# Sums of pooled keys and values move from GpSimd to TensorE, with another order of loads and steps, at the beginning of a fused attention and two-MoE kernel

## The chip, the core and the metric

The kernel runs on one core of one Trainium2 chip. The core has TensorE (PE: matmuls and the transposes made with an identity matrix), VectorE (DVE), ScalarE (ACT), GpSimd (POOL) and SyncE (SP), which here only issues DMAs in the order of its queue. The metric is the time of one execution in microseconds (us); lower is better.

## The reference, cut to what matters

```python
# q, k, v: 8 batches x 8 heads x 576 x 64, float32
k_p = k.reshape(B, H, 72, 8, D).mean(axis=3)      # keys and values averaged over 8 rows
v_p = v.reshape(B, H, 72, 8, D).mean(axis=3)
scores = (1 / sqrt(D)) * q @ k_p^T                # 576 x 72 for each head
attn = exp(scores - max) / (sum + 1e-9)
x = (attn @ v_p), heads side by side              # 4608 x 512
h = x @ w_in                                      # d_ff 2048, weights float64
x = (h * cos(h)) @ w_out
out = (silu(x @ w_gate) * (x @ w_val)) @ w_out2   # d_ff 1536
```

## The kernel before, in words

The kernel is one long instruction stream for each engine. Attention of batch 0 stands at the beginning; the first MoE runs over nine blocks of 512 tokens, and the attention of batches 1 to 7 is woven into its slots; the second MoE follows. A slot is one piece of 128 columns of the first MoE's d_ff: TensorE makes `h` (`pe_h`, L479 to L481), ScalarE and VectorE make h·cos(h) from it (`turns` and `cosine`; the last step is VectorE's `w`, L516), and TensorE adds it, two slots later, to `acc` (`pe_y`, L542 in block 0). Slot 0 of block 0 is called h_0 and w_0, and so on.

The weights come as float64 and are made into float32 on the chip. A unit (512 columns of 128 rows of `w_in`, or 128 rows of `w_out`) is loaded into `st_i` or `st_o` (L410) and goes through five VectorE steps: `cv_exp` (L417), `cv_sign` (L428), `cv_high` (L434), `cv_low` (L439) and `cv_mul` (L445); a unit of `w_in` has a sixth, the low part of `wa` (L959). (0,0) to (0,3) are the four units that h_0 to h_3 need, (1,0) to (1,3) those of h_4 to h_7, and so on. `fill(n)` puts n such steps into the stream; while block 0 runs, the converted units are consumed soon after they are made.

Attention of batch 0 goes over five tiles of up to 128 queries: `qT` (transposed queries, L241), scores `s` (TensorE, L253), their maximum `mx` (L257), `Exp` on ScalarE, `pm` (the normalized weights, L289 to L302), `pt` and `px` (their transposes on TensorE, L310, L314) with what VectorE makes of them, `ptl` (L312) and `ptx` (L316), and `av` (L330), whose result fills the `ring` that h_0 reads. `do_av` for group 0 (tiles 0 and 1) and group 1 (tiles 2 and 3) stand ahead of h_0.

The averages of 8 rows are sums of halves (`pool_sum`, L186 and L188: 8 rows to 4, to 2, to 1). Keys of batch 0 (`kst`) are summed on VectorE; values of batch 0 (`vst`, one tile of 128 x 5 x 512), keys and values of batch 1 (tiles `k_0`..`k_3`, `v_0`..`v_4`) and keys and values of all later batches (`kraw`, `vraw`, two buffers) on GpSimd. Sums give `kp` and `vp`; `prep_k` transposes `kp` into `kT`, `prep_v` splits `vp`.

The order of all this is written out by hand: a string `program` of steps for what is ahead of h_0 (s0 is `do_s` of tile 0, x0 its normalization, p0 `do_pt`, a0 `do_av` of group 0, m1 one GpSimd sum of batch 1, f4 four conversion steps, i1 and o1 a load of a unit, k and v `prep_k(1)` and `prep_v(0)`, X the split of the ring), and tables of slots after it.

Of the kernel before, what the change touches and what calls it, by code (L numbers as in the profile page):

```python
# [25 lines left out]
def fused_kernel(  # L26
# [216 lines left out]
    def do_s(b, t, e=None):  # L243
        n = TILES[t][1]
        qT = qTs.pop((b, t))
        if e is None:
            e = p1a.tile([P, H, SP], F32, name=f"e_{b}_{t}", tag="e")
        es[b, t] = e
        for hf in range(2):
            ps = psum.tile([P, 4, SP], F32, name=f"s_{b}_{t}_{hf}", tag="att", bufs=2)  # L250
            for j in range(2):
                p = 2 * hf + j
                nc.tensor.matmul(  # L253
                    ps[:n, 2 * j : 2 * j + 2].rearrange("p a b -> p (a b)"), qT[:, p], kT[:, p], start=True, stop=True
                )
# [755 lines left out]

    raw = iter(range(H + NP + 1))

    def more(m):
        for _ in range(m):
            i = next(raw, None)
            if i is not None:
                do_raw(1, i)
# [200 lines left out]
```

## Time and profile before

| what | us |
|---|---|
| median of 3 runs (1805.85 to 1807.25) | 1806.39 |
| the profiled execution | 1807.21 |
| its span, from the first to the last instruction | 1805.5 |
| TensorE busy in the span | 1721.2 (95%) |
| VectorE busy | 1284.0 (71%) |
| ScalarE busy | 1072.8 (59%) |
| GpSimd busy | 211.0 (12%) |

The profiled execution took 1.7 us more than its span, and 0.8 us more than the median. Busy shares are means over a kernel whose stretches differ: the first slices of the profile have TensorE busy at two to five tenths and VectorE at six to nine; from the fourth slice on TensorE stands at nine tenths or more. In the rows below, a name in square brackets behind an arrow is what ended the idle time before the instruction.

### The profile page before, as it was taken

How to read it: one execution, taken by the hardware profiler on the slowest of the kernel's cores; microseconds unless marked ns; L12 is line 12 of the kernel's file. 1: busy time of each engine (PE TensorE's matmuls, PEld its weight loads, DVE VectorE, ACT ScalarE, POOL GpSimd, SP SyncE). 2: the span in 40 equal slices, each digit the busy share in tenths (PEclk: the TensorE clock that was granted, in tenths of full speed). 3: DMA queues.
4: the chain of work that ended last, by engine and by line, in shares of the span. 5: the costliest groups of instructions: out<-in, count | busy, mean ns of one | idle time of the engine just before them, and what ended most of it. 6: DMA issues, size and time to landing. Idle time of an engine off the chain costs nothing.

```text
span 1805.5 us, 23613 instructions
## 1 busy us (share of the span) xinstructions
PE 1721.2 (95%) x8084; PEld 1443.0 (80%) x8084; DVE 1284.0 (71%) x2196; ACT 1072.8 (59%) x1947; POOL 211.0 (12%) x293
## 2 busy tenths in 40 slices
PE   2589999999999999999999999999999999999998
PEld 2455777788878888878878787888888888999998
DVE  6989988877777777787876586863584368358446
ACT  3567787777877777778676564533443344344333
POOL 4371423304104013000000000000000000000000
PEclk9699999999999999999999999999999999999999
DMA  9833356445656454574785488576667557777773
GB/s 188 182 104 92 102 180 196 147 137 180 169 178 224 135 192 138 165 230 150 235 272 178 153 322 288 192 249 228 197 199 268 189 196 219 293 261 248 293 251 93
DMA packets 248160, 357.04 MB, mean 198 GB/s; under 512 B 149608, under 2 KB 155752, under 8 KB 248040
## 3 DMA queue, kind: packets, MB, share of 16 engines
q1 hardware_dynamic: 224540, 351.99, 61.1%
q10 hardware_dynamic: 23500, 3.54, 1.4%
q8 instruction: 65, 1.06, 0.2%
q14 instruction: 55, 0.45, 0.1%
HBM read 285.74 MB, written 69.73 MB: 197 GB/s over the span
## 4 chain that ended last, share of the span: by engine, by line
PE 66%; DVE 18%; DMA 7%; ACT 6%; issue 2%; SPq 1%; POOL 0%; ACTq 0%; DVEq 0%; POOLq 0%
PE X L734 14%; PE oX L864 8%; PE Y L734 7%; PE acc L550 4%; PE acc L551 4%; PE oY L864 4%; PE acc L549 4%; PE h L479 4%; PE h L481 4%; PE h L480 4%; PE Z L734 3%; PE oZ L864 2%; DVE w L516 2%; DVE w L491 2%; PE av L330 1%
## 5 line engine op out<-in xcount | busy, mean ns | idle before, releaser
L479 PE MATMUL h<-xhl,wa 128*128 128x512 f32 x576 | 230.8, 401 | 5.6 <-ACT hs L488 5.6
L734 PE MATMUL X<-t_P,wc 128*128 128x512 f32 (+1 forms) x1080 | 233.5, 368 | 2.6 <-ACT u L783 2.5
L480 PE MATMUL h<-xhl,wa 128*128 128x512 f32 x576 | 226.6, 393 | 0.0
L481 PE MATMUL h<-xhl,wa 128*128 128x512 f32 x576 | 225.3, 391 | 0.0
L734 PEld LDWEIGHTS X<-t_P,wc 128*128 128x128 f32 x1080 | 196.3, 188 | 30.2 <-ACT u L783 5.2
L550 PE MATMUL acc<-gl,wo_ring 128*128 128x512 f32 x448 | 175.8, 392 | 2.3 <-DVE gl L530 2.3
L549 PE MATMUL acc<-gh,wo_ring 128*128 128x512 f32 x448 | 174.7, 400 | 1.0 <-ACT gh L527 0.9
L551 PE MATMUL acc<-gh,wo_ring 128*128 128x512 f32 x448 | 174.9, 390 | 0.0
L516 DVE SCALAR_TENSOR_TENSOR w<-w,hs 128x512 f32<-128x512 f32 x144 | 103.2, 716 | 45.7 <-ACT w L513 44.4
L479 PEld LDWEIGHTS h<-xhl,wa 128*128 128x128 f32 x576 | 108.7, 189 | 29.6 <-ACT hs L488 6.5
L512 ACT ACTIVATE w<-w 128x512 f32<-128x512 f32 x144 | 91.0, 632 | 67.3 <-DVE w L491 66.1
L488 ACT ACTIVATE hs<-h 128x512 f32<-128x512 f32 x144 | 85.7, 595 | 73.8 <-DVE w L516 49.9
L480 PEld LDWEIGHTS h<-xhl,wa 128*128 128x128 f32 x576 | 108.6, 189 | 23.8 <-issue 1.9
L481 PEld LDWEIGHTS h<-xhl,wa 128*128 128x128 f32 x576 | 108.6, 188 | 23.4 <-issue 0.7
L530 DVE TENSOR_TENSOR gl<-w,gh 128x512 fp32r<-128x512 f32 x133 | 96.5, 725 | 38.6 <-ACT gh L527 36.9
L786 DVE TENSOR_TENSOR p<-p,X 128x512 f32<-128x512 f32 (+1 forms) x60 | 37.8, 632 | 116.6 <-PE X L734 109.2
L491 DVE SCALAR_TENSOR_TENSOR w<-w,hs 128x512 f32<-128x512 f32 x144 | 106.3, 738 | 15.9 <-ACT w L490 15.7
L126 ACT CAST xhl<-pst 128x1024 fp32r<-128x1024 f32 (+1 forms) x70 | 67.7, 968 | 71.3 <-PE oX L864 26.1
L490 ACT ACTIVATE w<-hs,few 128x512 f32<-128x512 f32 x144 | 104.6, 726 | 6.2 <-DMA w_dram<-ce_w 4.8
L186 POOL TENSOR_TENSOR kraw<-kraw 72x256 f32<-72x256 f32 x96 | 85.4, 890 | 168.6 <-DMA kraw<-in_k_dram 164.8
L527 ACT CAST gh<-w 128x512 fp32r<-128x512 f32 x133 | 81.7, 615 | 35.6 <-DVE w L516 31.9
L864 PE MATMUL oX<-xhl,wc 128*128 128x512 f32 (+1 forms) x480 | 102.8, 368 | 0.0
(194 smaller groups left out, 3664.6 us busy)
## 6 DMA issues: line engine op xcount, KB each, us to landing
wc<-wc_dram SPq DMA_DIRECT2D x273, 512.0 KB
wo_ring<-wo_dram SPq DMA_DIRECT2D x112, 512.0 KB
wc_dram<-wc SPq DMA_DIRECT2D x42, 512.0 KB
wc_dram<-ow SPq DMA_DIRECT2D x42, 256.0 KB
y_dram<-yo SPq DMA_DIRECT2D x18, 512.0 KB
w_dram<-ce_w SPq DMA_DIRECT2D x36, 256.0 KB
st_i<-in_moe_w_in_dram SPq DMA_DIRECT2D x32, 256.0 KB
st_o<-in_moe_w_out_dram SPq DMA_DIRECT2D x16, 512.0 KB
```

Source lines behind the costliest of these rows:

```text
L479: nc.tensor.matmul(ps, whi, xhl[:, 0, c], start=c == 0, stop=False)
L480: nc.tensor.matmul(ps, whi, xhl[:, 1, c], start=False, stop=False)
L481: nc.tensor.matmul(ps, wlo, xhl[:, 0, c], start=False, stop=c == KC - 1)
L490: nc.scalar.activation(w, h, AF.Identity, bias=magic)
L491: nc.vector.scalar_tensor_tensor(out=w, in0=w, scalar=MAGIC, in1=h, op0=ALU.subtract, op1=ALU.subtract)
L516: nc.vector.scalar_tensor_tensor(out=w, in0=w, scalar=1.0, in1=h, op0=ALU.subtract, op1=ALU.mult, reverse0=True)
L530: nc.vector.tensor_sub(b, w, a)
L549: nc.tensor.matmul(acc[n][i], a[:, cols], xh, start=f == 0, stop=False)
L550: nc.tensor.matmul(acc[n][i], a[:, cols], xl, start=False, stop=False)
L551: nc.tensor.matmul(acc[n][i], b[:, cols], xh, start=False, stop=f == NF1 - 1)
L734: nc.tensor.matmul(ps[:, :hb], w, t[:, x, c, :hb], start=first and c == 0 and n == 0, stop=c == 1 and n == 2, skip_group_check=not first,)
L864: nc.tensor.matmul(banks[key][m][:, :hb], u, x[:, b, i, :hb], start=first_ and j == i == k == 0, stop=j == NJ - 1 and i == 1 and k == 2, s ...
```

## The change

- Values of batch 0 and keys and values of batch 1 are summed by TensorE: matmuls with the identity matrix, which add the eight pieces of 64 columns up in PSUM; ScalarE copies the sums out. In the program these are the steps V0, K and V; V0 stands between the scores of tile 0 and of tile 1, K and V between `av` of group 1 and the scores of tile 4. GpSimd's sums begin with batch 2 (`PEB = 2`).
- The keys get the factor −EXP_SCALE when `prep_k` copies them out of PSUM. So `mx` is a minimum instead of a maximum, the step that multiplied `mx` by −EXP_SCALE on VectorE is gone, and `Exp` has the scale −1.
- The loads have another order (unit (0,1) ahead of the queries, (0,2) ahead of the values of batch 0, (1,0) ahead of the keys of batch 1), and so has the program: conversions of (0,0) and (0,1) stand ahead of the first scores (`fill(6)`, `fill(14)`), conversions go on between the steps with other counts.

```diff
+    PEB = 2
     def load_kv1():
-            for r in range(2):
-                kvraw[1, "k", 2 * p + r] = t[:SP, r]
+            kraw.setdefault(1, []).append(t[:SP])
...
-        nc.scalar.copy(kT[0:64, :, 0:SP], ps[0:64])
-        nc.scalar.copy(kT[64:128, :, SP:], ps[64:128])
+        nc.scalar.mul(kT[0:64, :, 0:SP], ps[0:64], -EXP_SCALE)
+        nc.scalar.mul(kT[64:128, :, SP:], ps[64:128], -EXP_SCALE)
+
+    def sum_k1():
+        new_kp(1)
+        ps = psum.tile([SP, NP, 2, D], F32, name="kps_1s", tag="att", bufs=2)
+        for p, raw in enumerate(kraw[1]):
+            for l in range(POOL):
+                nc.tensor.matmul(
+                    ps[:, p].rearrange("s r d -> s (r d)"), ident[:SP, :SP], raw[:, :, l * D : (l + 1) * D],
+                    start=l == 0, stop=l == POOL - 1,
+                )
+        nc.scalar.copy(kps[1], ps)
+
+    def sum_v(b):
+        new_vp(b)
+        ps = psum.tile([P, NP + 1, D], F32, name=f"vps_{b}", tag="att", bufs=2)
+        for i, raw in vraw[b]:
+            m = raw.shape[1]
+            for l in range(POOL):
+                nc.tensor.matmul(
+                    ps[:, i : i + m].rearrange("p h d -> p (h d)"), ident, raw[:, :, l * D : (l + 1) * D],
+                    start=l == 0, stop=l == POOL - 1,
+                )
+        nc.scalar.copy(vps[b], ps)
...
-            nc.vector.reduce_max(mx[:n, :, 0], ps[:n], axis=AX.X)
+            nc.vector.tensor_reduce(out=mx[:n, :, 0], in_=ps[:n], op=ALU.min, axis=AX.X)
-                nc.vector.tensor_scalar_mul(mx[:n], mx[:n], -EXP_SCALE)
-                        e[:n, h], ps[:n, i], AF.Exp, bias=mx[:n, i], scale=EXP_SCALE, accum_out=sm[:n, h]
+                        e[:n, h], ps[:n, i], AF.Exp, bias=mx[:n, i], scale=-1.0, accum_out=sm[:n, h]
...
-    raws = [(b, kind, i) for b in range(1, B) for kind, m in (("k", H), ("v", NP + 1)) for i in range(m)]
+    raws = [(b, kind, i) for b in range(PEB, B) for kind, m in (("k", H), ("v", NP + 1)) for i in range(m)]
...
+    load_i(1)
     load_q(0)
     load_i(1)
...
+    fill(6)
     new_kp(0)
-    new_vp(0)
-    fill(1)
...
-    pool_sum(nc.gpsimd, vps[0], vst[:, : NP + 1])
+    fill(14)
...
-        "s0 s1 f4 m4 f5 s2 m4 x0 p0 m1 x1 f3 i1 p1 v s3 a0 m1 i1 m2 f12 o7 i2 x2 p2 m1 f5 x3 f4 s4 "
-        "f4 p3 a1 o3 i3 q F3 i1 k o4 X i4 x4 w f4 "
+        "s0 V0 s1 f4 i1 s2 x0 p0 x1 f3 p1 v s3 a0 f6 x2 p2 f3 x3 "
+        "f2 p3 a1 K V1 w i1 F3 X o2 s4 q i2 f8 x4 k b i4 f4 "
```

In the rows of the engines' order below, line numbers are those of each version (L280 of the changed kernel is L253 of before, L234 and L221 are the new sums).

TensorE at the first scores; `s_t_h` is the scores of tile t, half h, `vps` the sum of values of batch 0. Before:

```order
L209 MATMUL kps_159<-ident,kp_148 128x72 x4
L253 MATMUL s_0_0_172<-kT,qT_0_169 128x144 x2
L253 MATMUL s_0_1_183<-kT,qT_0_169 128x144 x2
L253 MATMUL s_1_0_195<-kT,qT_1_193 128x144 x2
L253 MATMUL s_1_1_206<-kT,qT_1_193 128x144 x2
```

Now:

```order
L211 MATMUL kps_170<-ident,kp_163 128x72 x4
L280 MATMUL s_0_0_204<-kT,qT_0_201 128x144 x2
L280 MATMUL s_0_1_214<-kT,qT_0_201 128x144 x2
L234 MATMUL vps_226<-vst,ident 128x320 x8
L280 MATMUL s_1_0_236<-kT,qT_1_223 128x144 x2
L280 MATMUL s_1_1_246<-kT,qT_1_223 128x144 x2
```

Eight matmuls of 320 columns, which need the values of batch 0, have come to stand ahead of the scores of tile 1.

TensorE between the last `av` of group 1 and the first matmuls of h_0. Before:

```order
L330 MATMUL av_1_3_542<-ptx,vl_97 128x256
L209 MATMUL kps_572<-ident,kp_226 128x72 x4
L479 MATMUL h_0_620<-xhl,wa_0_242 128x512
L480 MATMUL h_0_620<-xhl,wa_0_242 128x512
L481 MATMUL h_0_620<-xhl,wa_0_242 128x512
```

Now:

```order
L356 MATMUL av_1_3_462<-ptx,vl_97 128x256
L221 MATMUL kps_1s<-k_0_134,ident 72x128 x8
L221 MATMUL kps_1s<-k_1_136,ident 72x128 x8
L221 MATMUL kps_1s<-k_2_138,ident 72x128 x8
L221 MATMUL kps_1s<-k_3_140,ident 72x128 x8
L234 MATMUL vps_505<-v_0_142,ident 128x128 x8
L234 MATMUL vps_505<-v_2_145,ident 128x128 x8
L234 MATMUL vps_505<-v_4_148,ident 128x64 x8
L280 MATMUL s_4_0_549<-kT,qT_4_357 64x144 x2
L505 MATMUL h_0_627<-xhl,wa_0_179 128x512
L280 MATMUL s_4_1_559<-kT,qT_4_357 64x144 x2
```

All sums of batch 1 (56 matmuls) and the scores of tile 4 have come to stand ahead of h_0 or in its first matmuls; the transposes of the keys of batch 1 went behind its start.

SyncE's queue around the loads of `vraw` of batch 2 and `st_o_5` (the sixth unit of `w_out`). Before:

```order
L160 DMA kraw_7_1222<-in_k_dram 72x512
L163 DMA vraw_0_1280<-in_v_dram 64x512
L410 DMA st_o_4_427<-in_moe_w_out_dram 128x512
L163 DMA vraw_0_1280<-in_v_dram 64x512
L163 DMA vraw_1_1348<-in_v_dram 64x512 x2
L163 DMA vraw_2_1401<-in_v_dram 64x512 x2
L163 DMA vraw_3_1462<-in_v_dram 64x512 x2
L410 DMA st_o_5_429<-in_moe_w_out_dram 128x512
```

Now:

```order
L163 DMA kraw_7_1220<-in_k_dram 72x512
L436 DMA st_o_4_837<-in_moe_w_out_dram 128x512
L166 DMA vraw_0_1280<-in_v_dram 64x512 x2
L166 DMA vraw_1_1350<-in_v_dram 64x512 x2
L166 DMA vraw_2_1407<-in_v_dram 64x512
L436 DMA st_o_5_911<-in_moe_w_out_dram 128x512
L166 DMA vraw_2_1407<-in_v_dram 64x512
L166 DMA vraw_3_1470<-in_v_dram 64x512 x2
```

`st_o_5` now stands behind the first half of `vraw_2`, where it stood behind all of `vraw_3`; the two buffers of `vraw` make the load of `vraw_2` wait for GpSimd's sum of `vraw_0`, that of `vraw_3` for `vraw_1`.

## Rows read from the trace of the kernel before

**Rows 1.** Busy time of each engine by stretch; clock, DMA share, GB/s last.
```profile
core 0: us, PE busy (x) PEld busy (x) DVE busy (x) ACT busy (x) POOL busy (x), PEclk, DMA share, GB/s
28.00:62.00 34.00, 14.12 (x51) 10.96 (x51) 33.23 (x55) 14.34 (x58) 30.20 (x42) 0.94 0.90 176
62.00:82.00 20.00, 9.12 (x38) 7.65 (x39) 18.68 (x42) 10.69 (x35) 1.50 (x2) 0.50 1.03 222
...
140.00:215.00 75.00, 72.14 (x294) 48.50 (x293) 71.73 (x144) 62.26 (x149) 15.39 (x15) 1.00 0.35 96
215.00:1806.00 1591.00, 1572.37 (x7511) 1340.57 (x7509) 1095.33 (x1836) 936.75 (x1586) 125.10 (x181) 1.00 0.63 206
```

**Rows 2.** VectorE's groups by shape, 28 to 62 us: busy us, mean ns.
```profile
L439 DVE SCALAR_TENSOR_TENSOR st_i<-st_i 128x512 f32<-128x512 uint32 x3 | 6.0, 1997 | 0.0
...
L302 DVE COPY pm<-pm 128x64 f32<-128x64 f32 x1 | 2.1, 2060 | 0.0
```

**Rows 3.** The same view, 62 to 94 us.
```profile
L439 DVE SCALAR_TENSOR_TENSOR st_i<-st_i 128x512 f32<-128x512 uint32 x5 | 3.4, 682 | 0.0
...
L302 DVE COPY pm<-pm 64x64 f32<-64x64 f32 x1 | 0.2, 179 | 0.0
```

**Rows 4.** Timeline of GpSimd: start us, us, instructions.
```profile
28.80 4.49 POOL L186 TENSOR_TENSOR vst<-vst 128x1280 f32<-128x1280 f32 x2 [24.32 <-DMA vst<-in_v_dram]
...
117.14 9.56 POOL L186 TENSOR_TENSOR vraw<-vraw 128x256 f32<-128x256 f32 x2 [2.83 <-DMA vraw<-in_v_dram]
```

**Rows 5.** Timeline of VectorE.
```profile
16.77 0.68 DVE L428 SCALAR_TENSOR_TENSOR ce_i<-st_i,ce_i 128x512 uint32<-128x512 uint32 x1
...
78.06 0.68 DVE L439 SCALAR_TENSOR_TENSOR st_i<-st_i 128x512 f32<-128x512 uint32 x1
78.66 0.41 DVE L417 TENSOR_SCALAR wo<-st_o 128x512 uint32<-128x512 uint32 x1
79.00 0.68 DVE L445 SCALAR_TENSOR_TENSOR ce_i<-st_i,ce_i 128x512 f32<-128x512 f32 x1
...
92.70 0.69 DVE L516 SCALAR_TENSOR_TENSOR w<-w,hs 128x512 f32<-128x512 f32 x1
...
106.73 0.94 DVE L516 SCALAR_TENSOR_TENSOR w<-w,hs 128x512 f32<-128x512 f32 x1
...
134.15 0.43 DVE L417 TENSOR_SCALAR wo<-st_o 128x512 uint32<-128x512 uint32 x1 [5.19 <-DMA st_o<-in_moe_w_out_dram]
```

**Rows 6.** Timeline of TensorE.
```profile
76.31 0.58 PE L330 MATMUL av<-pth,vmh 128*128 128x256 f32 x1 [2.23 <-DVE ptl L312]
...
80.32 0.63 PE L330 MATMUL av<-ptx,vl 128*128 128x256 f32 x2
...
81.74 0.77 PE L479 MATMUL h<-xhl,wa 128*128 128x512 f32 x1
...
96.26 3.60 PE L542 MATMUL acc<-w,wo 128*128 128x512 f32 x8
...
107.73 6.19 PE L542 MATMUL acc<-w,wo 128*128 128x512 f32 x8 [4.14 <-DVE w L516]
...
136.52 0.79 PE L479 MATMUL h<-xhl,wa 128*128 128x512 f32 x1 [5.19 <-ACT hs L488]
```

**Rows 7.** Busy time and clock in three stretches that begin with a burst.
```profile
76.30:85.50 9.20, 8.85 (x32) 7.45 (x33) 8.29 (x18) 6.99 (x15) 0.32 (x1) 0.50 0.82 167
...
107.70:112.80 5.10, 5.07 (x6) 2.19 (x7) 5.10 (x7) 2.58 (x4) 4.86 (x6) 0.50 0.16 40
...
136.50:140.10 3.60, 3.25 (x4) 1.46 (x5) 3.57 (x7) 1.98 (x3) 2.89 (x4) 0.50 0.03 11
```

**Rows 8.** What SyncE's queue waited for, 0 to 200 us: total, times, longest.
```profile
SPq L410 <- DMA qi<-in_q_dram: 22.9, 2, 14.7
```

**Rows 9.** Timeline of SyncE's queue.
```profile
113.35 17.08 SPq L163 DMA_DIRECT2D vraw<-in_v_dram  x7
```

More of the change, by code (lines that the diff above doesn't have):

```diff
@@ L149, in fused_kernel @@
     kvraw = {}
+    kraw = {}
+    vraw = {}
     pairs = "(r p) (s l) d -> r s p (l d)"
@@ L179, in load_kv1 @@
                     nc.sync.dma_start(rows[:, 0], vleft[1])
-            for i in range(j, min(j + 2, NP + 1)):
-                kvraw[1, "v", i] = t[:, i - j]
+            vraw.setdefault(1, []).append((j, t[:, : min(2, NP + 1 - j)]))
     def pool_sum(eng, dst, raw):
@@ L205, in prep_k @@
     def prep_k(b):
+        ps = psum.tile([P, NP, SP], F32, name=f"kps_{b}", tag="att", bufs=2)
         kp = kps.pop(b)
-        ps = psum.tile([P, NP, SP], F32, name=f"kps_{b}", tag="att", bufs=2)
         for p in range(NP):
             nc.tensor.transpose(ps[:, p], kp[:, p].rearrange("s r d -> s (r d)"), ident[:SP, :SP])
-        nc.scalar.copy(kT[0:64, :, 0:SP], ps[0:64])
-        nc.scalar.copy(kT[64:128, :, SP:], ps[64:128])
+        nc.scalar.mul(kT[0:64, :, 0:SP], ps[0:64], -EXP_SCALE)
[21 more added lines that the diff above has]
+        nc.scalar.copy(vps[b], ps)
     def prep_v(b):
@@ L273, in do_exp @@
         e = es[b, t][: TILES[t][1]]
-        nc.scalar.activation(e, e, AF.Exp, scale=EXP_SCALE)
+        nc.scalar.activation(e, e, AF.Exp, scale=-1.0)
     def do_norm(b, t, pm=None):
@@ L337, in do_av @@
             done += m
-    raws = [(b, kind, i) for b in range(1, B) for kind, m in (("k", H), ("v", NP + 1)) for i in range(m)]
+    raws = [(b, kind, i) for b in range(PEB, B) for kind, m in (("k", H), ("v", NP + 1)) for i in range(m)]
     def do_raw(b, i):
-        at = (b - 1) * (H + NP + 1) + i
-        if at + 1 < len(raws) and raws[at + 1][0] > 1:
+        at = (b - PEB) * (H + NP + 1) + i
+        if at + 1 < len(raws):
             load_kv(*raws[at + 1])
@@ L979, in fused_kernel @@
     kst4 = kst[:SP].rearrange("s (p r) x -> s r p x", r=2)
+    vraw[0] = [(0, vst[:, : NP + 1])]
     load_i(1)
@@ L1010, in x_ @@
         do_norm(0, t, spare[t][:, NE:] if t % 4 else None)
[L1012 to L1018, printed above, removed]
     program = (
-        "s0 s1 f4 m4 f5 s2 m4 x0 p0 m1 x1 f3 i1 p1 v s3 a0 m1 i1 m2 f12 o7 i2 x2 p2 m1 f5 x3 f4 s4 "
-        "f4 p3 a1 o3 i3 q F3 i1 k o4 X i4 x4 w f4 "
+        "s0 V0 s1 f4 i1 s2 x0 p0 x1 f3 p1 v s3 a0 f6 x2 p2 f3 x3 "
+        "f2 p3 a1 K V1 w i1 F3 X o2 s4 q i2 f8 x4 k b i4 f4 "
     )
@@ L1030, in fused_kernel @@
         "v": lambda: prep_v(0),
-        "m": more,
+        "V": sum_v,
+        "K": sum_k1,
         "f": fill,
@@ L1037, in fused_kernel @@
         "k": lambda: prep_k(1),
+        "b": lambda: load_kv(*raws[0]),
         "w": lambda: wo_raw.extend(
```

## The prediction

> **What bounds the kernel now.** I read first the busy time by stretch [rows 1]. Beyond 215 us TensorE is busy for 1572.4 of 1591 us: an edit at the beginning changes nothing there, except by when that stretch starts. From 140 to 215 us TensorE still has 72.1 of 75. Ahead of it the picture turns: between 28 and 62 us VectorE is busy for 33.2 of 34 us and TensorE for 14.1; between 62 and 82 us VectorE for 18.7 of 20. So up to h_0, which starts at 81.74 us [rows 6], the time is VectorE's, and behind h_0 it is TensorE's with two holes in which it waits for VectorE: 4.14 us ahead of 107.73 for w_1, and 5.19 us ahead of 136.52 [rows 6].
>
> The groups by shape say why VectorE is full. A `cv_low` takes 1997 ns on the mean between 28 and 62 us and 682 ns after it; the copy of 64 columns in `pm` 2060 ns and 179 ns [rows 2, 3]. GpSimd is busy for 30.2 of the 34 us in the first stretch and for 1.5 of 20 in the next, where the DMA share is the higher one, 1.03 against 0.90 [rows 1]. So it is GpSimd's sums, not DMAs, that slow VectorE. Over all 55 instructions the excess over quiet steps comes to some 13 us (an estimate: of the two groups shown, 3.9 and 1.9).
>
> The Trainium skill states this as a rule (SBUF — State Buffer, section "SBUF: two separate sides"): VectorE and GpSimd share one port pair, the pair is locked for a whole instruction, and the loser blocks until it is over. Here the trace agrees: the 2060 ns copy lies under a GpSimd operation of 128x1280, two of which took 4.49 us [rows 4]. By the rule the sums of batch 2, which stay on GpSimd, will still slow VectorE in block 0; the sum below leaves that in by rows anyway.
>
> **The change, step by step, up to av of group 1.** I lay VectorE's new order out at quiet prices: a large step (L439 and its like) 0.60 us from start to start, a small one (L417) 0.34 [rows 5].
>
> - Keys of batch 0 are still summed first; today the next step starts at 16.77 [rows 5]. Then 8 large and 3 small conversion steps (5.8) lead to 22.6, the transposed queries to 23.2, and about 2.2 go by until the first scores and their minima are there. Of the 20 instructions that can run ahead of the scores of tile 1, 8.4 us in all, the last ends at 33.8.
> - These scores now stand behind V0. It needs the values of batch 0, which land at 28.80 [rows 4], and one more 512 KB unit is now loaded ahead of them: 2.6 us at some 200 GB/s (between the 176 and 222 of [rows 1]). So V0 starts at 31.4.
> - Price of V0: 8 x 320 = 2560 columns in float32. `acc` in block 0 is float32 too: four matmuls of 512 columns, each shown as two records, take 3.60 us [rows 6], so 1.76 ns a column at the full clock of 2.4 GHz; at the granted 0.50 that is 3.5. The clock is 0.50 from the start of a burst for 9.2, 5.1 and 3.6 us [rows 7]. If it rises 3.6 us after V0 begins, V0 takes 6.3; if not within it, 9.0. I take 7.5 (rise after the mean, 6 us): V0 ends at 38.9, the first half of the scores 1.0 later, and VectorE has waited for 6.1 us, which no row of today shows.
> - From there 61 instructions to the last `ptx` of tile 3: 23 large (13.8), 10 small (3.4), 28 others (7.7 at their quiet records), 24.9 in all. I add 1.5 for short waits on ScalarE and PSUM (today 2.1 idle in 54 us [rows 1]), and 2.3 for unit (2,3): its first step stands right ahead of `ptl` of tile 2, and its load stands on SyncE's queue behind a `kraw` that waits for the queries of batch 1, as loads do today for 22.9 us in two waits [rows 8]; I bound it by 0 and 6. `av` of group 1 starts at 68.6, today at 76.31 [rows 6]: **7.7 earlier.**
>
> **From there to h_0.** `av` takes 4.6 (76.31 to the last pair, whose second ends near 80.9 [rows 6]). Then K and V1: 32 x 128 + 16 x 128 + 8 x 64 = 6656 columns, 11.7 us at the full clock and 23.3 at half. The burst begins with `av`, so by [rows 7] the clock rises between 1 us before the sums and 4.6 us into them; a rise 1.4 in costs 0.7: 12.4. Scores of tile 4 and what stands with them: 0.7. h_0 starts at 86.3, **4.6 later than today.** The conversions, the ring's split and (2,3) that h_0 to h_3 need (10.6 us on VectorE) lie beside these sums. The ScalarE copies of the sums and the factor on the keys lie beside TensorE's work: nothing. If the conversions were late, h_0 would be late by the same amount; VectorE has some 7 us in hand there.
>
> **Behind h_0.**
> - h_0 starts at the full clock; today it ran at half from 81.74 to 85.5 [rows 6, 7]: −1.9.
> - The weights of tile 4 are made later, so `pt` of tile 4 may hold TensorE within h_1: +0.8 (an estimate between 0 and 1.6).
> - w_1. Today TensorE is ready for it at 103.6 and starts at 107.73. Now it is ready at 86.3 + 21.9 − 1.9 + 0.8 = 107.1. VectorE has 9.0 us of work from the scores of tile 4 to w_0, then today's 14.0 from w_0 to w_1 (92.70 to 106.73 [rows 5]; at quiet prices 10.3 before and after, and GpSimd's batch-2 keys still fall here), and 0.9 for w_1: 110.2. But units (2,0) to (2,2), whose steps stand ahead of w_0, now load into tiles that V1 frees only at 83 to 85 us; a load takes 3.6 us from the end of a queue's wait to its first step (130.4 to 134.15 [rows 5, 9]), so they come just in time or up to 2 us late: I take 1.0, 111.2. The hole stays at 4.1: 0.
> - `st_o`. VectorE waits 5.19 us at 134.15 for a unit of `w_out` [rows 5]; SyncE's queue had held it behind seven `vraw` for 17.08 us [rows 9], which waited for GpSimd, whose sum of the first `vraw` took 9.56 [rows 4]. In the new order it stands behind one and a half fewer `vraw`, and GpSimd comes to them without 5 batch-1 tiles in front and with two `kraw` half done: the unit lands some 10 us ahead of its need. What is late next is VectorE's own work, which TensorE doesn't wait for there. −5.2, and −1.8 for the half clock that followed (3.6 us at 0.50 [rows 7]): −7.0.
> - Without the waits, GpSimd's share and the removed scaling of `mx`, VectorE has 10.6 us less to do from w_1 to w_11. Of TensorE's 2.9 us idle between 140 and 215 [rows 1] half may go: −1.5.
>
> Sum: 4.6 − 1.9 + 0.8 + 0 − 7.0 − 1.5 = −5.0 against the profiled execution's 1807.2, so 1802.2. That execution stood 0.8 above the median, so the median of the changed kernel should be 1801.4.
>
> **A rule against it.** Today's clock is at half after each idle stretch and stays there for 3.6 to 9.2 us [rows 7]; a sum that stands in such a stretch costs twice its price. The Trainium skill (TensorE: Matmul & The Clock Gate, "Part 1: The HAM clock gate (the "warmup" mystery)") says that the default state is the throttled one and that activity releases it. By rows and rule V0 is dear, and this is in the sum; if the small matmuls of K (72x128) don't release it either, that is the first rival.
>
> **The rivals.**
> 1. *The sums of batch 1 stay at the half clock* (slower). Each is a short matmul between weight loads. Then K and V1 take 23.3 instead of 12.4, and h_0 gets no warm start: −5.0 + 10.9 + 1.9 = +7.8, 1814.2. It decides once the half clock lasts some 10 us further into the sums than I take, at half a microsecond lost for each. Against it: each of today's bursts rose within 9.2 us, the longest of them one of the same kind, `av`.
> 2. *The hole for `st_o` stays.* The unit still stands behind `vraw_0` and `vraw_1`, whose sums GpSimd makes slowly while VectorE runs without a gap (9.56 us [rows 4]). Then −5.0 + 7.0 = +2.0, 1808.4. For it: VectorE gets there sooner; against it: GpSimd is ahead of today by its batch-1 work.
> 3. *More of it is hidden.* VectorE's lead closes the hole at w_1 (−4.1), the half clock behind that hole (6.19 against 3.60 for the same eight records [rows 6], −2.6) and the rest of the idle time up to 215 us (−1.4): −13.1, 1793.3.
> 4. *GpSimd isn't what slows VectorE*, and the change doesn't free it. Then of the 13 us excess some 8 come back between tile 1 and `av`: −5.0 + 8 = +3.0, 1809.4. Against it stand the quiet prices at the higher DMA share [rows 1, 3].
>
> **How the numbers follow.** Chances: forecast 0.45 (its own range −9 to −1: V0, the wait for (2,3) and the clock at their ends, so 1797 to 1805), rival 1 0.12, rival 2 0.2, rival 3 0.18, rival 4 0.05. A measurement here tells 0.2%, 3.6 us, from no change. Of the forecast's cases three in four are faster than that, of rival 2's one in ten, all of rival 3's; slower by it are most of rival 1's, a quarter of rival 2's and half of rival 4's: faster 0.54, slower 0.17, same 0.29. The range goes from rival 3 to just short of rival 1: 1792 to 1811.
>
> **What would show it.** Right: `cv_low` and its like at 0.7 us between 28 and 62 us and GpSimd near idle there; V0 from 31 us, with VectorE waiting for the scores of tile 1 until 40; `av` of group 1 near 69; K and V1 in 12 us at a clock near 0.9, h_0 at 86; no wait for `st_o` near 130. Wrong: VectorE's steps still long without GpSimd; sums at 0.50 to their end; h_0 behind 92 us; the wait for `st_o` still there, or another load in its place ((2,3), or a piece of `w_in` that the new queue has put back).

## The result, and the profile of the changed kernel

The changed kernel takes 1820.57 us (median of 4 runs, 1818.19 to 1825.21), the kernel before 1806.82 (4 runs, 1805.85 to 1807.83): ratio 1.0079 [1.0058, 1.0101]. It is slower by 0.8%, some 14 us; the prediction said 1801.4 and is wrong, and the time lies outside its range. The profiled execution of the changed kernel took 1825.21, the longest of the four.

Busy time by stretch, with the columns of [rows 1]; 82 to 108 and 205 to 245 us are stretches that [rows 1] does not have:

```profile
28.00:62.00 34.00, 20.77 (x75) 15.66 (x75) 28.16 (x66) 19.25 (x79) 0.00 (x0) 0.75 0.96 202
62.00:82.00 20.00, 9.90 (x43) 9.03 (x44) 11.21 (x22) 7.00 (x15) 2.67 (x4) 0.51 0.33 68
82.00:108.00 26.00, 26.00 (x140) 23.62 (x139) 11.89 (x27) 8.19 (x28) 0.60 (x2) 0.72 0.60 149
140.00:215.00 75.00, 70.33 (x285) 46.53 (x283) 61.23 (x118) 57.49 (x137) 17.53 (x28) 0.98 0.33 90
...
205.00:245.00 40.00, 35.91 (x160) 27.34 (x161) 37.39 (x63) 27.58 (x55) 21.66 (x27) 1.00 0.32 101
```

The last of these in the kernel before:

```profile
205.00:245.00 40.00, 39.21 (x182) 32.06 (x181) 36.61 (x60) 31.59 (x56) 26.84 (x35) 1.00 0.47 157
```

GpSimd, the fifth engine, is idle from 28 to 62 us, and VectorE has room: it is busy for 28.16 of 34 us with more instructions than before (66 against 55). VectorE's groups by shape in that stretch answer to [rows 2]:

```profile
L465 DVE SCALAR_TENSOR_TENSOR st_i<-st_i 128x512 f32<-128x512 uint32 x5 | 3.5, 692 | 0.1
...
L328 DVE COPY pm<-pm 128x64 f32<-128x64 f32 x1 | 0.2, 186 | 0.0
```

692 and 186 ns, where [rows 2] had 1997 and 2060: without GpSimd beside them both groups have their quiet price. That part came as predicted. TensorE's timeline (L234 and L221 are the sums, L505 is h, L568 `acc` in block 0, L575 and L577 `acc` behind it):

```profile
31.60 6.21 PE L234 MATMUL vps<-vst,ident 128*128 128x320 f32 x16 [5.22 <-DVE pm L322]
...
73.33 0.58 PE L356 MATMUL av<-pth,vmh 128*128 128x256 f32 x1 [3.31 <-DVE ptl L338]
...
78.22 13.93 PE L221 MATMUL kps_1s<-k,ident 72*72 72x128 f32 x64 [0.25 <-ACT ring L362]
91.94 7.60 PE L234 MATMUL vps<-v,ident 128*128 128x128 f32 x48
...
100.11 0.50 PE L505 MATMUL h<-xhl,wa 128*128 128x512 f32 x1
...
124.66 6.61 PE L568 MATMUL acc<-w,wo 128*128 128x512 f32 x8 [3.50 <-DVE w L542]
...
226.96 0.50 PE L575 MATMUL acc<-gh,wo 128*128 128x512 f32 x1 [2.38 <-ACT wo L522]
229.38 0.96 PE L577 MATMUL acc<-gh,wo 128*128 128x512 f32 x3 [0.54 <-DVE wo L555]
233.20 0.97 PE L577 MATMUL acc<-gh,wo 128*128 128x512 f32 x3 [0.63 <-DVE wo L555]
```

`av` of group 1 starts at 73.33 and not at 68.6; K takes 13.93 us, and h_0 starts at 100.11, 18.4 later than in [rows 6] and 13.8 later than predicted. The clock (the third number from the end) in four stretches of the sums:

```profile
82.00:86.00 4.00, 4.00 (x21) 4.00 (x20) 4.00 (x9) 0.00 (x0) 0.00 (x0) 0.50 0.48 131
...
94.00:96.00 2.00, 2.00 (x12) 2.00 (x11) 0.01 (x1) 0.00 (x0) 0.00 (x0) 0.50 0.00 0
96.00:98.00 2.00, 2.00 (x18) 2.00 (x18) 0.00 (x0) 0.00 (x0) 0.00 (x0) 0.90 0.48 129
98.00:99.50 1.50, 1.50 (x15) 1.43 (x14) 0.00 (x0) 0.00 (x0) 0.00 (x0) 1.00 0.78 216
```

From 78.2 us on TensorE is busy without a gap worth naming (17.78 of the 17.80 us to 96), and it has the half clock, 1.2 GHz, until 96 us, 23 us after `av` began. VectorE's timeline shows two waits for loads, and the wait of 5.19 near 134 [rows 5] gone:

```profile
67.46 0.43 DVE L443 TENSOR_SCALAR wo<-st_i 128x512 uint32<-128x512 uint32 x1 [5.40 <-DMA st_i<-in_moe_w_in_dram]
...
151.73 0.43 DVE L443 TENSOR_SCALAR wo<-st_o 128x512 uint32<-128x512 uint32 x1 [2.25 <-DMA st_o<-in_moe_w_out_dram]
```

Up to here the profile shows a late h_0. But the lateness doesn't stay the same. VectorE's last step `w` of each slot of 128 columns, counted on from w_0, against that of before, in the profiled executions (start minus start, us; the last column is the change from w_13 to w_18; the rows behind the second are the experiments below):

| run | w_0 | w_4 | w_9 | w_13 | w_18 | w_23 | w_13 to w_18 |
|---|---|---|---|---|---|---|---|
| before, at | 92.7 | 135.1 | 175.3 | 202.2 | 236.3 | 268.1 | |
| changed | +18.1 | +11.3 | +9.7 | +6.4 | +20.2 | +19.0 | **+13.8** |
| e1_sums_on_gpsimd | +6.0 | +5.9 | +2.1 | −2.1 | +9.4 | +8.8 | **+11.5** |
| e2_values_first | +10.8 | +12.6 | +3.0 | +2.8 | +12.0 | +9.6 | **+9.2** |
| e3_sums_in_the_wait | +19.4 | +17.3 | +13.5 | +9.4 | +21.0 | +22.2 | **+11.6** |
| e6_order_only | +12.5 | +12.0 | +8.2 | +4.2 | +15.8 | +16.8 | **+11.6** |
| e8_before_late_loads | +1.9 | −0.1 | +0.2 | −2.8 | +10.3 | +8.9 | **+13.1** |
| e4_w_out_loads_early | +9.7 | +8.3 | +0.4 | −0.8 | +0.3 | −0.6 | +1.1 |
| e11_late_asked_early | +9.6 | +2.2 | −0.1 | +1.4 | +0.9 | +0.5 | −0.5 |
| e9_gpsimd_early_loads | +7.3 | +5.3 | +1.5 | +3.0 | +3.9 | +4.2 | +0.9 |
| e13_values_first_asked_early | +11.3 | +13.6 | +3.9 | +4.4 | +6.3 | +6.9 | +1.9 |
| e5_sums_only | +11.5 | +7.9 | +5.2 | +4.3 | +8.6 | +8.6 | +4.3 |
| e7_queries_on_sync | −1.7 | −23.0 | +2.8 | +1.8 | −0.2 | +4.6 | −1.9 |
| e10_values_first_on_sync | 0.0 | −23.2 | −0.8 | +1.3 | +2.7 | +3.8 | +1.4 |
| e12_keys_early_on_sync | −3.8 | −11.4 | +4.8 | +3.4 | +4.0 | +4.0 | +0.7 |

Of the 18.1 us, 11.7 have been made good by w_13, behind h_0 as predicted; a part of that is work put off, as the conversions below show. Then 13.8 are lost again between 208 and 257 us, for the most part in a stretch of which the prediction says that the beginning changes nothing. SyncE's queue shows what is late there:

```profile
199.52 7.07 SPq L163 DMA_DIRECT2D kraw<-in_k_dram  x4
215.04 0.35 SPq L436 DMA_DIRECT2D st_o<-in_moe_w_out_dram  x1
...
217.78 0.35 SPq L436 DMA_DIRECT2D st_o<-in_moe_w_out_dram  x1
...
228.25 0.54 SPq L436 DMA_DIRECT2D st_o<-in_moe_w_out_dram  x1
```

The last three of the 16 units of `w_out` are issued among and behind the last six loads of batch 3's keys. In the kernel before, the last two units went out together, ahead of those six:

```profile
194.06 3.07 SPq L410 DMA_DIRECT2D st_o<-in_moe_w_out_dram  x2
197.66 20.03 SPq L160 DMA_DIRECT2D kraw<-in_k_dram  x6
```

VectorE's last conversion step of the last unit, before and now:

```profile
206.70 0.68 DVE L445 SCALAR_TENSOR_TENSOR wo<-st_o,wo 128x512 f32<-128x512 f32 x1
...
237.04 0.67 DVE L471 SCALAR_TENSOR_TENSOR wo<-st_o,wo 128x512 f32<-128x512 f32 x1
```

From w_13 to w_18, before and now:

```profile
202.15:236.28 34.13, 33.34 (x156) 27.32 (x155) 32.16 (x52) 26.51 (x49) 24.93 (x27) 1.00 0.38 126
...
208.58:256.51 47.93, 42.52 (x190) 32.71 (x189) 44.38 (x75) 33.72 (x62) 23.21 (x29) 1.00 0.43 147
```

Before, 2 units were converted behind w_13; now it is 5, and VectorE has 75 instructions from w_13 to w_18 where it had 52, busy for 44.38 of 47.93 us. So the delay reads as more work for VectorE in this stretch, and hardly as a wait: VectorE's longest wait for one of these units in the changed kernel is 0.45 us. The first two of the five were issued between 184.60 and 192.17 us; why their steps stand behind w_13 all the same no run here separates from the late requests.

### The profile page after: what moved, and what is told of

Same layout as the page of the kernel before. It is cut to its first block, busy times and chain, and to the rows that moved or that the text cites. A ratio compares the mean times of both kernels' runs of the same rounds, so it can differ in the third digit from the quotient of the medians.

```text
span 1823.4 us, 23787 instructions
## 1 busy us (share of the span) xinstructions
PE 1743.4 (96%) x8212; PEld 1465.4 (80%) x8212; DVE 1267.6 (70%) x2176; ACT 1072.5 (59%) x1950; POOL 173.5 (10%) x251
## 4 chain that ended last, share of the span: by engine, by line
PE 69%; DVE 12%; DMA 8%; ACT 6%; issue 2%; POOL 2%; SPq 1%; ACTq 0%; DVEq 0%; POOLq 0%
PE X L760 14%; PE oX L890 8%; PE Y L760 7%; PE h L505 4%; PE h L507 4%; PE h L506 4%; PE acc L576 4%; PE acc L577 4%; PE acc L575 4%; PE oY L890 4%; PE Z L760 3%; PE oZ L890 2%; PE av L356 2%; PE s L280 1%; DMA st_i<-in_moe_w_in_dram 1%
## 5 line engine op out<-in xcount | busy, mean ns | idle before, releaser
L505 PE MATMUL h<-xhl,wa 128*128 128x512 f32 x576 | 231.5, 402 | 2.7 <-ACT hs L514 2.6
L575 PE MATMUL acc<-gh,wo_ring 128*128 128x512 f32 x448 | 174.5, 400 | 0.7 <-ACT gh L553 0.7
L577 PE MATMUL acc<-gh,wo_ring 128*128 128x512 f32 x448 | 174.8, 390 | 0.0
L505 PEld LDWEIGHTS h<-xhl,wa 128*128 128x128 f32 x576 | 108.3, 188 | 27.7 <-ACT hs L514 3.6
L517 DVE SCALAR_TENSOR_TENSOR w<-w,hs 128x512 f32<-128x512 f32 x144 | 104.3, 724 | 17.7 <-ACT w L516 17.7
```

Source lines behind the costliest of these rows:

```text
L505: nc.tensor.matmul(ps, whi, xhl[:, 0, c], start=c == 0, stop=False)
L517: nc.vector.scalar_tensor_tensor(out=w, in0=w, scalar=MAGIC, in1=h, op0=ALU.subtract, op1=ALU.subtract)
L575: nc.tensor.matmul(acc[n][i], a[:, cols], xh, start=f == 0, stop=False)
L577: nc.tensor.matmul(acc[n][i], b[:, cols], xh, start=False, stop=f == NF1 - 1)
```

## The experiments

The first theory was that the sums cost it all: they stand ahead of h_0 at the half clock. Its rival was the order of loads and steps, whatever engine sums. From the fourth run on, the rival had a place: the program string asks for 2 units of `w_out` ahead of the slots (`o2`), where before it asked for 14 (`o7`, `o3`, `o4`); the others are asked for one by one as earlier ones are converted. No run leaves out any of the work. Each median stands with its range and number of runs, each ratio is to the kernel before, with its 95% interval.

**Sums of batch 1 back on GpSimd** (`e1_sums_on_gpsimd`), the rest of the change kept:

```diff
+            for r in range(2):
+                pool_sum(nc.gpsimd, kps[1][:, p, r], raw[:, r])
...
+                for j in range(raw.shape[1]):
+                    pool_sum(nc.gpsimd, vps[b][:, i + j], raw[:, j])
...
-        "s0 V0 s1 f4 i1 s2 x0 p0 x1 f3 p1 v s3 a0 f6 x2 p2 f3 x3 "
-        "f2 p3 a1 K V1 w i1 F3 X o2 s4 q i2 f8 x4 k b i4 f4 "
+        "s0 V0 s1 K V1 f4 i1 s2 x0 p0 x1 f3 p1 v s3 a0 f6 x2 p2 f3 x3 "
+        "f2 p3 a1 w i1 F3 X o2 s4 q i2 f8 x4 k b i4 f4 "
```

> Only the sums of batch 1 go back to GpSimd (they start there as their loads land); V0, the scaled keys, the loads and the program stay as changed. Theory 1 (the 21 us of K and V1 at the half clock ahead of h_0 are the loss): h_0 comes some 20 us sooner, less what GpSimd's port costs VectorE between 35 and 60 us (up to 8 us), so h_0 at 80 to 88 us and 1801 to 1809 us in all. Theory 2 (the loss is in the new order: the wait of 5.4 us for unit (2,3) and other loads that come late): the waits stay, h_0 near 95, 1815 or more.

It takes 1818.0 us (1815.74 to 1820.32, 6 runs), ratio 1.0058 [1.0043, 1.0073]. h_0 starts at 86.41, 13.7 us ahead of the profiled execution of the changed kernel, yet the medians are only 2.6 us apart, and from w_13 to w_18 this one loses 11.5 as well. So the sums of batch 1 ahead of h_0 are not what makes the change slower. The start of h_0 is what its theory 1 expected, the time what its theory 2 did.

**Values first** (`e2_values_first`): K and V1 change places.

```diff
-        "f2 p3 a1 K V1 w i1 F3 X o2 s4 q i2 f8 x4 k b i4 f4 "
+        "f2 p3 a1 V1 K w i1 F3 X o2 s4 q i2 f8 x4 k b i4 f4 "
```

> V1 ahead of K instead of behind it, nothing else. Theory A (matmuls that use 72 rows and 72 columns of the array, K, don't release the clock, those with 128 rows, V1, do): the clock rises 4 to 5 us after V1 begins; if K then keeps it, both take 13 to 14 us instead of 21.3, h_0 starts near 93 and the total is near 1813. If K drops the clock again, K takes up to 13.7 and V1 6.7: about 1820. Theory B (the clock rises a fixed time after the burst began, whatever runs): sums of 21 us as before, 1820.

It takes 1821.9 us (1817.25 to 1824.67, 6 runs), ratio 1.0074 [1.0057, 1.0091]. TensorE's timeline:

```profile
79.50 5.59 PE L234 MATMUL vps<-v,ident 128*128 128x128 f32 x48 [0.25 <-ACT ring L362]
84.93 7.16 PE L221 MATMUL kps_1s<-k,ident 72*72 72x128 f32 x64
```

Here the sums take 12.6 us, close to the predicted 12.4, and the time is the changed kernel's all the same. The half clock isn't the main cause either.

**The sums in TensorE's wait** (`e3_sums_in_the_wait`): K and V1 moved up, behind `pt` of tile 2.

```diff
-        "s0 V0 s1 f4 i1 s2 x0 p0 x1 f3 p1 v s3 a0 f6 x2 p2 f3 x3 "
-        "f2 p3 a1 K V1 w i1 F3 X o2 s4 q i2 f8 x4 k b i4 f4 "
+        "s0 V0 s1 f4 i1 s2 x0 p0 x1 f3 p1 v s3 a0 f6 x2 p2 K V1 f3 x3 "
+        "f2 p3 a1 w i1 F3 X o2 s4 q i2 f8 x4 k b i4 f4 "
```

> K and V1 stand between the transposes of tile 2 and of tile 3, where TensorE waited 8.2 us for VectorE (which waited for unit (2,3)) and 3.3 us more. Theory 1 with the half clock kept: sums from 60 to 81 us, tile 3 some 12 us late, h_0 near 92, total near 1812. Theory 1 with a clock that rises during V1: sums end near 79, h_0 near 90, 1810. Theory 2 (the wait for the load and the new order are the loss, the sums are covered): no gain from the place, 1818 to 1822.

It takes 1828.29 us (1827.39 to 1829.15, 4 runs), ratio 1.0113 [1.0097, 1.0129], more than either theory expected. TensorE, and then VectorE:

```profile
70.25 13.93 PE L221 MATMUL kps_1s<-k,ident 72*72 72x128 f32 x64 [8.38 <-DVE ptl L338]
```

```profile
69.17 0.43 DVE L443 TENSOR_SCALAR wo<-st_i 128x512 uint32<-128x512 uint32 x1 [7.39 <-DMA st_i<-in_moe_w_in_dram]
92.33 0.43 DVE L443 TENSOR_SCALAR wo<-st_i 128x512 uint32<-128x512 uint32 x1 [18.22 <-DMA st_i<-in_moe_w_in_dram]
```

The idle stretch could not be filled: K itself waited 8.38 us for `ptl` of tile 2, which stands behind (2,3) on VectorE and, as I read it, gives back the PSUM buffer that K's sums take; and VectorE then waited 18.22 us for a further unit. Again K took 13.93 us.

**The same order with all sums on GpSimd** (`e6_order_only`): V0, K and V1 of the changed kernel are `pool_sum` on GpSimd, and K and V1 stand where GpSimd comes to them early.

```diff
+                pool_sum(nc.gpsimd, vps[b], raw)
...
-        "s0 V0 s1 f4 i1 s2 x0 p0 x1 f3 p1 v s3 a0 f6 x2 p2 f3 x3 "
-        "f2 p3 a1 K V1 w i1 F3 X o2 s4 q i2 f8 x4 k b i4 f4 "
+        "s0 V0 K V1 s1 f4 i1 s2 x0 p0 x1 f3 p1 v s3 a0 f6 x2 p2 f3 x3 "
+        "f2 p3 a1 w i1 F3 X o2 s4 q i2 f8 x4 k b i4 f4 "
```

> The changed kernel with all sums on GpSimd, V0's too, as before (they start as their data land); the new loads, program and scale stay. Theory 1: without sums on TensorE the loss is gone, 1804 to 1810. Theory 2: the wait for unit (2,3) and the late w_out units stay, 1814 to 1820.

**The sums alone** (`e5_sums_only`): the kernel before with V0, K and V1 on TensorE, its own order of loads, its maximum and its 14 units.

```diff
-        "s0 s1 f4 m4 f5 s2 m4 x0 p0 m1 x1 f3 i1 p1 v s3 a0 m1 i1 m2 f12 o7 i2 x2 p2 m1 f5 x3 f4 s4 "
-        "f4 p3 a1 o3 i3 q F3 i1 k o4 X i4 x4 w f4 "
+        "s0 V0 s1 f4 f5 s2 x0 p0 x1 f3 i1 p1 v s3 a0 i1 f12 o7 i2 x2 p2 f5 x3 f4 s4 "
+        "f4 p3 a1 K V1 o3 i3 q F3 i1 k o4 X b i4 x4 w f4 "
```

> The kernel before with the sums on TensorE alone (V0 between the scores of tiles 0 and 1, K and V1 behind av of group 1, no GpSimd steps of batch 1); loads, conversions' counts, the maximum and the scale stay as before. Theory 1 (the sums are the loss): h_0 some 10 us later than 81.7, total 1813 to 1822. Theory 2 (the new order of loads and steps is the loss): VectorE gains its quiet prices, w_out's loads stay early, and the total is 1800 to 1808.

Order only takes 1823.28 us (1817.97 to 1827.05, 6 runs), ratio 1.0084 [1.0069, 1.0098], 3 us above what was expected for the rival; sums alone take 1814.9 us (1813.23 to 1818.06, 5 runs), ratio 1.0043 [1.0031, 1.0055]. The order alone, with its 2 units, costs as much as the whole change. The sums alone cost about half of it, and lose 4.3 us from w_13 to w_18, where all versions that ask for 2 units lose 9 to 14. What they cost isn't the late loads: `e5_sums_only` asks for its 14 units and converts 2 behind w_13, as the kernel before does. Its time lies in the range that was expected if the sums were the loss, and what makes it slower in the old order of steps is not shown here.

**Twelve more units asked for early** (`e4_w_out_loads_early`):

```diff
-        "f2 p3 a1 K V1 w i1 F3 X o2 s4 q i2 f8 x4 k b i4 f4 "
+        "f2 p3 a1 K V1 w i1 F3 X o14 s4 q i2 f8 x4 k b i4 f4 "
```

> The changed kernel with one number changed: the program asks for 14 units of w_out ahead of h_0 (as the kernel before does in three steps) instead of 2, so that units 11 to 15 stand ahead of batch 3's keys in SyncE's queue and not between them. Theory 2 (the gain behind h_0 is given back at the end of block 0, because units 13 to 15 arrive at 215 to 230 us and VectorE converts them beside w_14, w_15 and batch 2): w_16's delay against before no longer grows from +8 to +20 us, the last conversion ends near w_13 as before, and the total falls by 4 to 10 us, to 1811 to 1817. Theory 1 (the whole loss stands ahead of h_0, in the sums at the half clock): 1819 to 1822, no change.

It takes 1806.54 us (1802.8 to 1816.97, 11 runs), ratio 0.9995 [0.9981, 1.0008]: two characters give back 14 us, where 4 to 10 were expected. TensorE's busy time where the loss was, and the sums of this profiled execution (1802.8):

```profile
205.00:245.00 40.00, 40.00 (x190) 33.37 (x189) 35.42 (x60) 32.33 (x60) 22.80 (x30) 1.00 0.48 157
```

```profile
78.22 7.21 PE L221 MATMUL kps_1s<-k,ident 72*72 72x128 f32 x64 [0.69 <-ACT ring L362]
85.26 5.47 PE L234 MATMUL vps<-v,ident 128*128 128x128 f32 x48
```

40.00 of 40 us instead of 35.91. And by chance it shows a second thing: `av` and K start at the same 73.33 and 78.22 as in the changed kernel, with the same instructions ahead of them, but here the clock rose within `av`, before K, and the same matmuls took 7.21 and not 13.93.

**The loss put into the kernel before** (`e8_before_late_loads`): the kernel before, with 2 units asked for instead of 14 and nothing else.

```diff
-        "s0 s1 f4 m4 f5 s2 m4 x0 p0 m1 x1 f3 i1 p1 v s3 a0 m1 i1 m2 f12 o7 i2 x2 p2 m1 f5 x3 f4 s4 "
-        "f4 p3 a1 o3 i3 q F3 i1 k o4 X i4 x4 w f4 "
+        "s0 s1 f4 m4 f5 s2 m4 x0 p0 m1 x1 f3 i1 p1 v s3 a0 m1 i1 m2 f12 o2 i2 x2 p2 m1 f5 x3 f4 s4 "
+        "f4 p3 a1 i3 q F3 i1 k X i4 x4 w f4 "
```

> The kernel before with one thing undone: its program asks for 2 units of w_out ahead of h_0 instead of 14; sums, conversions, scale stay. Theory 2 (late w_out units at the end of block 0 are the loss): units 11 to 15 are converted behind w_13 as in the changed kernel, block 1 starts 8 to 14 us late, total 1814 to 1822. Theory 1 (only the sums and what stands ahead of h_0 matter): 1806 to 1809.

It takes 1815.85 us (1811.71 to 1822.18, 7 runs), ratio 1.0043 [1.0026, 1.006]. VectorE waits for the last unit and TensorE for VectorE, with the largest hole that any version has between 205 and 245 us:

```profile
226.77 0.44 DVE L417 TENSOR_SCALAR wo<-st_o 128x512 uint32<-128x512 uint32 x1 [6.23 <-DMA st_o<-in_moe_w_out_dram]
```

```profile
227.99 1.22 PE L551 MATMUL acc<-gh,wo 128*128 128x512 f32 x2 [7.06 <-DVE wo L529]
```

```profile
205.00:245.00 40.00, 30.85 (x128) 24.98 (x129) 33.21 (x57) 24.31 (x40) 25.15 (x25) 0.91 0.38 125
```

So the late requests alone make the kernel before slower, in the same stretch: the cause is shown from both sides. The count of conversions agrees in all runs: every version that asks for 2 units converts 5 of the 16 behind w_13 and begins the last step between 229 and 242 us; every version that asks for 14 converts 1 or 2 there and begins it between 205 and 218.

**GpSimd's sums with the early units** (`e9_gpsimd_early_loads`) is e1 with `o14`; **asked for at the end of the program** (`e11_late_asked_early`) leaves `o2` and adds the twelve behind everything else, so that VectorE's order ahead of h_0 is that of the changed kernel:

```diff
-        "f2 p3 a1 K V1 w i1 F3 X o2 s4 q i2 f8 x4 k b i4 f4 "
+        "f2 p3 a1 K V1 w i1 F3 X o2 s4 q i2 f8 x4 k b i4 f4 o12 "
```

> The kernel with the early w_out loads, and the sums of batch 1 back on GpSimd (as in the run with sums on GpSimd). It prices those sums with the loads right: if TensorE's sums cost 6 to 12 us ahead of h_0 and VectorE's quiet prices give that back, 1804 to 1808, the same as with sums on TensorE; if the sums are a net loss, 1800 to 1804; if a net gain, 1809 or more.

> The changed kernel with one step appended to its program (o12: the other 12 units of w_out are asked for at its end, behind everything else), so that what stands ahead of w_3 keeps the changed kernel's order and only the later w_out loads move ahead of batch 3's keys. Theory 2 (the late units 11 to 15 alone make the loss at the end of block 0): 1806 to 1810, near the run with all 14 asked for. If the other effect of that run counted (units 2 to 5 converted ahead of w_0): 1813 to 1818. Theory 1: 1819 to 1822.

The first takes 1808.59 us (1806.5 to 1813.69, 12 runs), ratio 1.0005 [0.9994, 1.0016], the second 1805.98 (1804.5 to 1818.03, 12 runs), ratio 1.0000 [0.9984, 1.0016]. The two places tried for the requests, in e4 and in e11, take the same time; in both the last unit goes out ahead of the last six keys of batch 3. And with them, sums of batch 1 on TensorE and on GpSimd take the same time.

**The queries of batch 1 on SyncE's queue** (`e7_queries_on_sync`), to take away the wait for (2,3); `e10_values_first_on_sync` is that with V1 ahead of K, and `e12_keys_early_on_sync` that with the first keys of batch 2 asked for ahead of the splits, and with `o2` and `o12`:

```diff
-    ACT_QUEUE = {(0, 0), (3, 1), (1, 1), (3, 0), (1, 0)}
+    ACT_QUEUE = {(0, 0), (3, 1), (3, 0)}
...
-        "f2 p3 a1 K V1 w i1 F3 X o2 s4 q i2 f8 x4 k b i4 f4 "
+        "f2 p3 a1 K V1 w i1 F3 X o14 s4 q i2 f8 x4 k b i4 f4 "
```

> The kernel with the early w_out loads (1806.5 us), and the queries of batch 1 issued by SyncE instead of ScalarE, so that no load in SyncE's queue waits for a piece that ScalarE has not issued yet; unit (2,3)'s first step then no longer stands ahead of tile 2's ptl on VectorE. If the wait of 5.3 us for that unit sets when h_0 starts: h_0 some 5 us sooner than 91.0, total 1801 to 1804. If something else arrives just as late (the queries' 11 us of issue on SyncE hold up units of w_in, or the hole at w_1 takes the gain): 1805 to 1809.

> As the run with the queries on SyncE, with V1 ahead of K. If V1 releases the clock and K keeps it, the executions that stay at the half clock through K (10 us longer, 1 in 11 of the run with early loads) are gone and the rest is the same: median equal to that of the other run within 1.5 us, smaller spread.

> The queries of batch 1 on SyncE (h_0 near 81 us, as in that run), the first load of batch 2's keys ahead of the w_out loads, and w_out asked for in two steps (2, then 12 at the end). In the run with the queries on SyncE a lead of 23 us at w_4 was gone at w_5, GpSimd's sums fell into 140 to 260 us and VectorE had to convert w_in units late. If GpSimd's late sums ate the lead, they now come earlier and the total is 1801 to 1805; if VectorE's own work up to block 1 is the bound (its conversions only move), 1806 to 1810.

They take 1809.6 us (1808.3 to 1811.43, 12 runs), ratio 1.0007 [0.9998, 1.0015]; 1809.39 (1805.42 to 1811.81, 12 runs), 1.0006 [0.9995, 1.0018]; and 1815.15 (1807.48 to 1819.85, 12 runs), 1.0032 [1.0017, 1.0047]. The wait for (2,3) is gone, `av` of group 1 starts at 63.06 in the first, and w_4 is 23 us ahead of before. Then 18 of the 23 us are lost within one slot and the rest by w_8:

```profile
137.43 1.11 PE L336 MATMUL pt<-ident,pm 128*128 128x128 f32 x4 [7.22 <-ACT e L290]
...
141.79 0.79 PE L505 MATMUL h<-xhl,wa 128*128 128x512 f32 x1 [2.68 <-ACT hs L514]
```

```profile
108.00:140.00 32.00, 23.25 (x92) 14.46 (x90) 30.79 (x61) 23.77 (x73) 11.06 (x14) 0.91 0.55 135
140.00:215.00 75.00, 69.22 (x270) 47.15 (x271) 72.36 (x132) 58.59 (x131) 29.78 (x28) 0.92 0.40 107
```

VectorE is busy for 30.79 of 32 and 72.36 of 75 us, and GpSimd's sums of batch 2 stand later, 29.78 us of them from 140 to 215 where the changed kernel has 17.53. TensorE came early to a stretch that VectorE's work bounds, and its lead was worth nothing here; the `e` that it waits for comes from ScalarE, which had itself waited 2.67 us for VectorE just before. Earlier keys of batch 2 (e12) did not help: its 1815.15 lies above both of the ranges that were expected, and why it is slower than the other two is not shown. Values first (e10) did not narrow the executions as expected: they spread over 6.4 us, those of e7 over 3.1.

**Values first, late units mended** (`e13_values_first_asked_early`), for the half clock: e11 with `V1 K`.

> The changed kernel with the late units of w_out asked for early (as in the run that appended one request of twelve units at the program's end, 1805.98 us), and with V1 ahead of K: first the matmuls with 128 rows, then those with 72. If the short 72-row matmuls of K are what sometimes keeps the clock at half through the sums, no execution of this one is about 10 us above its median (that run had two in twelve: 1812.9 and 1818.0), the granted clock is at least 0.986 in all, and the median is within 3 us of 1806. If the half clock is drawn anew in any execution whichever sums stand first, one or two in twelve are again 7 to 12 us longer at a clock near 0.982. With V1 first the ring's split and the conversions are not touched, so h_0 stays near 91 to 93 us in the profile at the full clock, and the late units stay early: no requests of w_out behind the keys of batch 3.

It takes 1814.31 us (1812.88 to 1819.39, 6 runs), ratio 1.0038 [1.0025, 1.0052]. The expected median was missed by 8 us. The sums are not the reason (V1 6.13, K 7.16); the wait for `st_o` has come back, and with it a hole:

```profile
136.09 0.43 DVE L443 TENSOR_SCALAR wo<-st_o 128x512 uint32<-128x512 uint32 x1 [5.48 <-DMA st_o<-in_moe_w_out_dram]
```

```profile
137.26 2.26 PE L280 MATMUL s<-kT,qT 128*128 128x144 f32 x8 [6.33 <-DVE ptl L338]
```

The unit was issued at 132.15, in e11 at 127.37, each time behind `vraw` that wait for GpSimd: in these two executions rival 2 hangs on 5 us of GpSimd's pace. That this wait is the whole of the 8 us is not shown. None of the six executions stands 10 us above the median; six are too few to settle that (below).

## Why the prediction was wrong

- **What failed: "an edit at the beginning changes nothing there, except by when that stretch starts", said of the time beyond 215 us.** I priced the loads up to `st_o_5` and left out that the new program asks for 2 units of `w_out` where it asked for 14, though this stands in the diff. So the end of block 0 had no term in the sum. The runs show in its place that the last three units are issued among batch 3's keys and that five are converted behind w_13. Measured: 13.8 us from w_13 to w_18; 14.0 and 14.6 us between the medians of the changed kernel and those of e4 and e11; 13.1 us from w_13 to w_18 when put into the kernel before, of which 0.43%, 7.8 us, are left in its ratio. The 13.8 and 13.1 overstate the loss, since at w_13 these versions have 11 units converted and the kernel before has 14: e8's lead of 2.8 us at w_13 is such work put off.
- **The rise of the clock: rival 1 was real, but a draw.** In the changed kernel's profiled execution K ran at half, 13.93 us, and so did half of V1: h_0 at 100.11; with the same start e4 had 91.29. That is 8.8 of the 22.4 us between these two executions; I put the rest down to the late loads. The other three executions of the changed kernel (1818.19 to 1821.42) have a mean clock of 0.986 to 0.988, the profiled one 0.982, which suggests that the median holds little of it; they have no trace. Two of the signs that the prediction gave for being wrong came, h_0 behind 92 us and the wait for (2,3), but neither is where the time went: e1 has h_0 at 86.41 and takes 1818.0.
- **`av` of group 1, "7.7 earlier", came 3.0 earlier.** V0 was right in its start (31.60 for 31.4) and shorter than taken (6.21 for 7.5; the prediction gave 6.3 for an early rise of the clock). From there VectorE was idle for 9.1 of the 36 us from 38 to 74 (26.87 busy), where the sum had 1.5 for short waits and 2.3 for (2,3); (2,3) alone took 5.40, within its bounds.
- **The sums were right where the clock rose early, in part by luck**: from `av` of group 1 to h_0 17.7 us were predicted (68.6 to 86.3), and e4 shows 18.0 (73.33 to 91.29). Of the predicted 12.4 for K and V1, 11.7 were their price at the full clock and 0.7 a late rise; in e4 the clock had risen before them and they took 12.5 (78.22 to 90.73).
- **Behind h_0** the sum had −9.6 (−1.9, +0.8, 0, −7.0, −1.5); e4 goes from +9.7 at w_0 to −0.8 at w_13; its terms were not measured one by one. The hole at w_1 stayed (3.50 us for 4.14; in e4 it is one slot later, 3.31). The wait of 5.19 for `st_o_5`, near 134, is gone in the changed kernel, e2, e4, e5 and the three with the queries on SyncE, and down to 0.87 in e11. So rival 2 was real too: e13 has 5.48 of it, and e1, e3, e6 and e9 have 2.6 to 3.8, three of which sum batch 1 on GpSimd.
- **Rival 4 fell**: VectorE's prices are quiet where GpSimd is idle (692 and 186 ns). The trace agrees with the Trainium skill's rule of the locked port pair (SBUF — State Buffer, "SBUF: two separate sides").
- **What stays.** With the loads mended no version is measurably faster than before (0.9995, 1.0000, 1.0005), against a forecast of −5.0. In the sum the late `av` is 4.7 of that; but e7 has no wait for (2,3) and `av` at 63.06, and gained nothing: by its trace VectorE's work up to 215 us was the next bound. So the step from an earlier or later h_0 to the end of the kernel, which the sum takes one for one, failed as well. No version here is measurably faster than the kernel before.

## What to carry to other kernels

In a hand-written order the counts of requests are as much a part of the change as the moved work: for each stream of loads, list where each request stands before and after in the queue that issues it, to the last one, also far behind the place that is edited. A late start can be made good behind it and an early start lost, so follow the delay slot by slot before naming a cause: the slot where it changes is the place, not the first one where it is large. And check that a profiled execution is near the median before its longest operation is blamed.

## What was not expected of the hardware

The clock rose at different points in executions with the same instructions up to there. In e4 it rose within `av`, some 3.5 us after this began (0.81 from 76.0 to 78.2); in the changed kernel TensorE, busy with hardly a gap from 73.33, stayed at 0.50 until 96 us, through all of K, and so it did in e3 (0.50 from 70.3 to 84.0, and until some 3 us into V1). Where the clock had risen before K or in its first microsecond (e2, e4, e5, e7, e10 to e13) K took 7.15 to 7.45 us; where it hadn't, 13.93, twice, and the rise came some 3.4 and 4.5 us into V1. The Trainium skill (TensorE: Matmul & The Clock Gate, "Part 1: The HAM clock gate (the "warmup" mystery)") says that the point differs from run to run of one kernel. The traces agree on that, with some 20 us between the changed kernel and e4, which is far more than the page tells of; K's 13.93 us at 0.50 are longer than any burst of [rows 7]. Executions 5 to 12 us above the median at a mean clock of 0.982 or 0.983 are 3 of 27 with K first (the changed kernel, e4, e11) and none of 12 with V1 first (e2, e13); with e7, e12 and e10, whose queries are on SyncE, it is 3 of 51 and none of 24. That doesn't separate the two; whether K's short matmuls hold the clock down stays open.
